# Router logits with the gates stationary in column groups, later low halves of x, and feed-forward low halves on DVE

## The chip, the core and the metric

The kernel runs on one core of a Trainium2 chip. The metric is device time in microseconds (us) for one launch, median of several runs. The engines are named as the profile names them: PE (matrix multiply), PEld (its weight load), DVE, ACT, POOL and SP (which issues most of the DMAs).

## What is computed

Three layers follow each other, and each needs the one before in full:

```python
# attention: 4 batches, 8 heads, 576 positions, head size 64
scores = scale * q @ k.T + bias            # bias: a small network on relative positions
attn = exp(scores - max) / sum
x = (attn @ v)                             # -> 2304 tokens x 512
# experts: one of 8 by the router
logits = x @ w_gate; e = argmax(logits)
gate = softmax(logits)[e] * sigmoid(x @ w_output_gate)[e]
x = gate * (relu(x @ w1[e]) @ w2[e])
# feed forward
g = x @ w_gate; out = (silu(g) * (x @ w_val)) @ w_out      # 512 -> 1536 -> 512
```

Everything is float32. Many products run as three products of halves: a float32 value a is cut into a high half h (rounded to the short format fp32r, one ACT copy) and a low half l = a - h (one subtraction), and a*b is computed as ah*bh + ah*bl + al*bh.

## The kernel before

**Attention** runs 16 units (head pair p, batch b), each of 5 steps over row pieces of 128 positions. A step makes scores on PE (line 251), the bias addition on DVE (255), the exponential on ACT (260), the transposes of the probabilities E on PE (274), their copies `pt` out of PSUM on ACT (279) and DVE (281), and the product with v on PE (336), whose result is scaled into `xT`. Units run with the batch innermost; the last head pair of batch 0 is finished in unit 13 or so, so the **router** of batch 0 can be threaded into the steps of units 14 and 15.

**The router** of batch b is a list of functions: logits (x times both gate matrices, 16 columns), `shift`, `gates`, `spread` and `first`. A table of numbers (`LG` for batch 0, `SP0` and `MC` for the first cuts of x and of the first expert weights) says at which step each function is called. For batch 0 the logits are 20 plain float32 products with x stationary and the gates moving, 16 columns wide (line 372). For the batches 1 to 3 they are 16 products of halves with `wgr`, the cut gates, stationary and 288 columns of x moving (387), then five narrow transposes (397), and an addition of the two halves. `gates` ends in two reciprocals, a maximum and three products on DVE (416 to 421), whose result `ex` is what `spread` transposes on PE (428). `first` finds the expert of the batch, `e0i`, with which SP loads that expert's weights (502, 503).

**Experts:** 4 blocks (one per batch) of 16 steps. A step is 12 products with the first weight (`T`, line 553), relu and cut (ACT 555, DVE 556), and 12 products with the second (`y`, 566). After steps 7 and 15 DVE scales four tiles of y into `yo` (575). A dictionary `todo` lists which other function is called at the end of which step: for batch b, with n = 16b - 15, router function i at step n + 4 + i//2, loads of the expert's weights from n + 7 on, their cuts (ACT 517, DVE 518) from n + 9 on. The step with the scaling of the first eight is n + 6.

**Feed forward:** five token chunks (four of 512, one of 256), each of 12 steps. In a step `gv` makes 24 products (line 1183, g and v), silu on ACT and two products on DVE (1185 to 1187), and cuts the result t into `uh` (ACT 1190) and `ul` (POOL 1191); `outs` makes the 12 products of an output piece (1205) per 128 tokens. The weights come as 36 pieces of 128 x 512 in a 64-bit format. `narrow_w` turns each into float32 and cuts it in three stages: `expo` (ACT 938), `bits` (three DVE operations, 941 to 943), `halves` (high half on ACT 946, low half on POOL 947). Pieces 0 to 5 are converted during the last expert block, pieces 6 to 35 during the steps of chunk 0, three a step, by `more_w`, which calls `cv_w` once a piece; `cv_w` runs one stage of every piece in its queue, oldest first.

All engines work through their own instructions in program order, so the order in which these functions are called is the order on each engine.

Of the kernel before, what the change touches and what calls it, by code (L numbers as in the profile page):

```python
# [21 lines left out]
NP = H // 2  # L22
# [12 lines left out]
LG = (3, 3, 5, 5, 7, 7, 8, 10, 10)  # L35
# [4 lines left out]
MC, SP0 = ((17, 18), 9)  # L40
# [67 lines left out]
def body(tc, qt, kt, va, vb, ws, moe_w_gate, moe_w_output_gate, moe_w1, moe_w2, w_gate, w_val, w_out, ctab, cst, cst2, out):  # L108
    nc = tc.nc
    with ExitStack() as ctx:  # L110
# [24 lines left out]
        wg = const.tile([128, 4, 16], F32, name="wg")  # L135
        wgr = const.tile([128, 224], F32R, name="wgr")
# [219 lines left out]
        def router(b):  # L356
# [7 lines left out]
            def logits_early(c):  # L364
                def f():
                    if c == 0:
                        t["ps"] = pO.tile([128, 512], F32, tag="pv", bufs=2, name="lps")
                        nc.gpsimd.memset(tl("lg", [128, 5, 16])[64:128, 4], 0.0)
                    ps, lg = t["ps"], t["lg"]
                    n = 64 if c == 4 else 128  # L370
                    for p in range(NP):
                        nc.tensor.matmul(ps[0:n, 16 * c:16 * c + 16], xT[p][:, b * S + 128 * c:b * S + 128 * c + n], wg[:, p],
                                         start=p == 0, stop=p == NP - 1)
                    if c == 4:
                        nc.scalar.activation(lg[:, 0:4], ps[:, 0:64].rearrange("p (c e) -> p c e", e=16), AF.Copy)
                        nc.scalar.activation(lg[0:64, 4], ps[0:64, 64:80], AF.Copy)
                return f

            def logits():

                ps = [pO.tile([128, 512], F32, tag="pv", bufs=2, name="lps") for _ in range(2)]
                t["raw"] = ap.tile([128, S], F32, tag="rb" if b else "E", bufs=1 if b else 4, name="lraw")[0:32]
                for f in range(2):
                    o = slice(288 * f, 288 * f + 288)
                    for p in range(NP):
                        for i in range(2):
                            nc.tensor.matmul(ps[f][:, 0:288], wgr[:, 32 * p:32 * p + 128], mu[b]["xs"][p][i][:, o],
                                             start=p == 0 and i == 0, stop=p == NP - 1 and i == 1)
                    nc.scalar.activation(t["raw"][:, o], ps[f][0:32, 0:288], AF.Copy)

            def logits_t():
                ps = pO.tile([128, 512], F32, tag="pv", bufs=2, name="lps")
                lg = tl("lg", [128, 5, 16])
                nc.gpsimd.memset(lg[64:128, 4], 0.0)
                for c in range(5):
                    n = 64 if c == 4 else 128
                    nc.tensor.transpose(ps[0:n, 32 * c:32 * c + 32], t["raw"][:, 128 * c:128 * c + n], ident[0:32, 0:32])
                for n, c in ((128, slice(0, 4)), (64, slice(4, 5))):
                    v = ps[0:n, 0:160].rearrange("p (c e) -> p c e", e=32)[:, c]
                    nc.scalar.activation(lg[0:n, c], v[:, :, 0:16], AF.Copy)  # L400
                    nc.vector.tensor_tensor(lg[0:n, c], v[:, :, 16:32], lg[0:n, c], ALU.add)
# [47 lines left out]
            return ([logits, logits_t] if b else [logits_early(c) for c in range(5)]) + [shift, gates, spread, first]  # L449
# [56 lines left out]
        def conv_w(raw, f):  # L506
# [9 lines left out]
            for x, y in ((a, ta), (cc, tb)):  # L516
                nc.scalar.activation(y[:, 0], x, AF.Copy)
                nc.vector.tensor_tensor(y[:, 1], x, y[:, 0].bitcast(F32), ALU.subtract)
# [228 lines left out]
        def m_conv(b, f):  # L747
            mu[b]["ws"][f] = conv_w(mu[b]["raw"][f], f)
# [20 lines left out]
        def consts():  # L769
            nc.sync.dma_start(cst_sb, cst)  # L770
            nc.sync.dma_start(wg[:, :, 0:8], moe_w_gate.rearrange("(p d) e -> d p e", p=4))
            nc.sync.dma_start(wg[:, :, 8:16], moe_w_output_gate.rearrange("(p d) e -> d p e", p=4))

        def gate_halves():
            w = wgr[:, 0:128].rearrange("p (k i e) -> p k i e", k=4, i=2)
            nc.scalar.activation(w[:, :, 0], wg, AF.Copy)
            nc.vector.tensor_tensor(w[:, :, 1], wg, w[:, :, 0].bitcast(F32), ALU.subtract)
            nc.vector.tensor_scalar(wgr[:, 128:224], ident[:, 0:96], 0.0, None, ALU.mult)
        extra.insert(len(extra) - 6, consts)
        extra.append(gate_halves)  # L780
# [149 lines left out]
        def narrow_w(n, r, t):  # L930
# [26 lines left out]
        def early_cv(n):  # L957
# [11 lines left out]
            return expo, lambda: fs[1](), lambda: fs[2]()  # L969


        p_recip(sts[15])
        late.pop()()
# [69 lines left out]
        for i in range(2):  # L1043
            t_ev(*a[0:3], t_pe(a[3], a[2], i), i)
            pvs(2)
# [69 lines left out]
        with ExitStack() as c2:  # L1115
# [39 lines left out]
            def cv_w(n):  # L1155
# [10 lines left out]
                for q in list(cvq):  # L1166
                    q.pop(0)()
                if cvq and not cvq[0]:
                    cvq.pop(0)

            us = {}

            def gv(j, f):
# [17 lines left out]
                nc.gpsimd.tensor_tensor(ul, t, uh.bitcast(F32), ALU.subtract)  # L1191
# [51 lines left out]
            def more_w(n):  # L1243
                for m in range(MW(n), min(MW(n + 1), 3 * NF + 2)):
# [3 lines left out]
                    cv_w(m)  # L1248
                for _ in range(FL):
# [3 lines left out]
            for n, (j, f) in enumerate(steps):  # L1253
# [5 lines left out]
                if j == 0:  # L1259
                    more_w(f)  # L1260
                if f == NF - 2 and j + 1 < NCH:
# [24 lines left out]
```

## Time and profile before

| | us |
|---|---|
| median of 3 runs (lowest to highest) | 1089.32 (1085.95 to 1091.72) |
| the profiled execution | 1090.41 |
| its span in the trace | 1088.6 |
| attention, units 0 to 13 (69.80 to 289.33) | 219.53 |
| attention, unit 14 (289.33 to 315.35) | 26.02 |
| attention, unit 15 and the hand-over (315.35 to 345.03) | 29.68 |
| feed forward, chunk 0 up to its last step (609.40 to 733.13) | 123.73 |
| feed forward, 35 steps behind it (733.13 to 1020.00) | 286.87 |

Over the span the granted TensorE clock is 0.969 of full speed, PE is busy 94%, DVE 52%, ACT 42%, POOL 20%. These shares are averages over stages with different limits. The stage tables give, for a stretch, the busy time of each engine; the waits view sums what an engine waited for; the timeline gives single instructions with their start and duration.

### The profile page before, as it was taken

To read this page: it belongs to the slowest core of one execution; us is meant where nothing else is said; L and a number is where in the kernel's file an instruction comes from. 1 tells how busy PE (TensorE), PEld (TensorE's weight loads), DVE (VectorE), ACT (ScalarE), POOL (GpSimd) and SP (SyncE) were. 2 spreads that over 40 slices of the span, in tenths; PEclk is the share of its full clock that TensorE was granted. 3 is DMA by queue.
4 is the path that set the end of the run, shared out by engine and by line. 5 is a ranking of instruction groups with operands and counts; after the bars stand their busy time and mean duration, and the time that the engine had idled before them with its cause. 6 is when DMAs were issued, how large, how long until landed. Compare 5 with 4: busy or idle time off the path is not lost. (4 is left out here: it accounts for less than half of the span.)

```text
span 1088.6 us, 19099 instructions
## 1 busy us (share of the span) xinstructions
PE 1027.2 (94%) x7544; PEld 818.5 (75%) x7544; DVE 562.4 (52%) x1225; ACT 457.9 (42%) x1034; POOL 217.3 (20%) x212
## 2 busy tenths in 40 slices
PE   7979999999988999999998888889999999999998
PEld 2347666666765899999998666668888888888897
DVE  8966677767645554545655599971112211211211
ACT  6766777777644433333444344442112111211221
POOL 2112333323300000000020155541111111111111
PEclk9988999999978999999999899999999999999999
DMA  6773342333012241734733544422000100100010
GB/s 191 208 249 105 95 126 84 98 115 102 2 29 71 69 156 55 278 107 130 247 120 135 188 136 155 136 77 78 1 1 20 58 1 1 58 1 1 1 39 20
DMA packets 67758, 101.94 MB, mean 94 GB/s; under 512 B 9136, under 2 KB 37936, under 8 KB 67664
## 3 DMA queue, kind: packets, MB, share of 16 engines
q1 hardware_dynamic: 67504, 100.41, 28.8%
q8 instruction: 61, 1.00, 0.4%
q14 instruction: 33, 0.27, 0.1%
q10 hardware_dynamic: 160, 0.26, 0.1%
HBM read 74.63 MB, written 26.03 MB: 92 GB/s over the span
## 5 line engine op out<-in xcount | busy, mean ns | idle before, releaser
L1183 PE MATMUL v<-x,w 128*128 128x512 f32 (+1 forms) x720 | 166.2, 379 | 16.8 <-POOL w L947 16.1
L1183 PEld LDWEIGHTS v<-x,w 128*128 128x128 f32 x720 | 128.3, 193 | 46.2 <-POOL w L947 20.4
L1183 PE MATMUL g<-x,w 128*128 128x512 f32 (+1 forms) x720 | 158.8, 369 | 2.4 <-DVE x L1146 1.5
L1186 DVE TENSOR_TENSOR t<-g,t 128x512 f32<-128x512 f32 (+1 forms) x60 | 38.2, 636 | 226.1 <-ACT t L1185 226.1
L1183 PEld LDWEIGHTS g<-x,w 128*128 128x128 f32 x720 | 126.7, 188 | 27.5 <-DVE x L1146 3.0
L1191 POOL TENSOR_TENSOR ul<-t,uh 128x512 fp32r<-128x512 f32 (+1 forms) x60 | 72.6, 1211 | 333.0 <-ACT uh L1190 333.0
L1205 PE MATMUL o<-w,uh 128*128 128x512 f32 x432 | 134.5, 393 | 0.0
L260 ACT ACTIVATE E<-E,st 128x576 f32<-128x576 f32 x144 | 110.6, 774 | 4.8 <-DVE st L255 4.4
L274 PEld LDWEIGHTS T<-ident,E 64*128 64x128 f32 x1312 | 67.6, 145 | 58.5 <-ACT pt L279 26.4
L336 PE MATMUL pv<-pt,rawv 128*64 128x256 f32 (+1 forms) x640 | 103.3, 437 | 1.3 <-DVE xT L342 1.3
L274 PE MATMUL T<-ident,E 64*128 64x64 f32 x1312 | 94.3, 243 | 9.4 <-DVE pt L281 4.0
L255 DVE CUSTOM_DVE_ANT_0 E<-S,bias 128x576 f32<-128x576 f32 x128 | 92.0, 755 | 18.9 <-PE S L251 10.8
L1185 ACT ACTIVATE t<-g 128x512 f32<-128x512 f32 (+1 forms) x60 | 33.1, 551 | 155.4 <-PE g L1183 155.4
L1190 ACT ACTIVATE uh<-t 128x512 fp32r<-128x512 f32 (+1 forms) x60 | 35.4, 589 | 146.1 <-DVE t L1187 146.1
L1205 PEld LDWEIGHTS o<-w,uh 128*128 128x128 f32 x432 | 81.4, 190 | 16.6
L281 DVE COPY pt<-T 128x256 f32<-128x256 f32 x160 | 59.6, 414 | 61.0 <-PE T L274 61.0
L279 ACT ACTIVATE pt<-T 128x320 f32<-128x320 f32 (+1 forms) x160 | 56.0, 392 | 70.2 <-PE T L274 67.8
L1205 PE MATMUL o<-w,ul 128*128 128x512 f32 x216 | 84.7, 392 | 0.0
L251 PE MATMUL S<-kh,qz 64*128 64x288 f32 (+1 forms) x576 | 79.6, 327 | 3.6 <-DVE st L255 3.1
L555 ACT ACTIVATE qz<-T 128x288 fp32r<-128x288 f32 x63 | 25.9, 411 | 103.7 <-PE T L553 103.7
L556 DVE SCALAR_TENSOR_TENSOR qz<-T,qz 128x288 fp32r<-128x288 f32 x63 | 28.8, 457 | 75.7 <-ACT qz L555 75.6
L1187 DVE TENSOR_TENSOR t<-v,t 128x512 f32<-128x512 f32 (+1 forms) x60 | 38.3, 638 | 55.6 <-PE v L1183 54.2
(246 smaller groups left out, 1741.3 us busy)
## 6 DMA issues: line engine op xcount, KB each, us to landing
raww<-in_moe_w_dram SPq DMA_DIRECT2D x16, 768.0 KB, 6.1
bscr<-ob SPq DMA_DIRECT2D x36, 288.0 KB, 3.6
bias<-bscr SPq DMA_DIRECT2D x16, 576.0 KB, 4.6
rw<-in_w_gate_dram SPq DMA_DIRECT2D x12, 512.0 KB, 3.6
rw<-in_w_val_dram SPq DMA_DIRECT2D x12, 512.0 KB, 3.6
rw<-in_w_out_dram SPq DMA_DIRECT2D x12, 512.0 KB, 3.7
rawq<-in_qt_dram SPq DMA_DIRECT2D x16, 320.0 KB, 3.3
rawk<-in_kt_dram SPq DMA_DIRECT2D x16, 288.0 KB, 2.8
```

The lines of the kernel that those rows point to most:

```text
L251: nc.tensor.matmul(t[:, f, 0:288], x[k, a], y[k, o], start=i == 0, stop=i == 2)
L255: nc.vector.tensor_tensor_reduce(out=E.rearrange("p (a b) -> p a b", a=2), in0=ps[:, :, 0:288], in1=bt[p, hh, c].rearrange("p (a b) -> p a ...
L260: nc.scalar.activation(E, E, AF.Exp, bias=st[:, 2 * c + hh:2 * c + hh + 1], scale=-1.0, accum_out=st[:, 10 + 2 * c + hh:11 + 2 * c + hh])
L274: nc.tensor.transpose(t[r][:, 64 * j:64 * j + 64], E[k, o:o + 128], ident[k, k])
L279: nc.scalar.activation(o, x, AF.Copy)
L281: nc.vector.tensor_copy(o, x)
L336: nc.tensor.matmul(st["ps"][64 * hh:64 * hh + 64, 0:w], vt[p][:, hh, b, c, :], pts[p, b][f][:, c + (5 * hh if c < 4 else 0), :], start=c = ...
L1183: nc.tensor.matmul(t, a[:, 128 * k:128 * k + 128], x, start=k == 0 and n == 0, stop=k == 3 and n == 2)
L1186: nc.vector.tensor_tensor(t, ps[0], t, ALU.mult)
L1187: nc.vector.tensor_tensor(t, ps[1], t, ALU.mult)
L1191: nc.gpsimd.tensor_tensor(ul, t, uh.bitcast(F32), ALU.subtract)
L1205: nc.tensor.matmul(ops[j][m], u[:, o], w, start=f == 0 and n == 0, stop=f == NF - 1 and n == 2)
```

## The change

Three things are changed.

**Router.** One set of functions serves all batches. The logits are 8 plain float32 products: the gates of head pair p (16 columns, filled with zeros to 32) are stationary, 288 columns of x move, and the four head pairs write into four groups of 32 PSUM partitions. ACT copies 128 partitions twice, PE transposes five 128 x 128 pieces, and DVE adds up the four groups with two reductions. The cut gates `wgr` and their three instructions are gone. `gates` is cut into `gates` and `gates_2`; with seven functions instead of six, batches 1 to 3 run `gates_2` and `spread` at step n + 6 and `first` at n + 7. For batch 0 the table now puts the logits into step 0 of unit 14.

**First cuts of x.** The cuts of x of batch 0 are called one step later (`SP0`), the low halves of the first expert weight are put off into a list, and that list and the reciprocal of the last unit are called between the two halves of the transposes behind unit 15.

**Feed forward.** The low halves of weight pieces and of the products u are subtracted on DVE instead of POOL. A piece has four stages, and `cv_w` runs: high half of piece m-2 (ACT), bits of m-1 (DVE), low half of m-2 (DVE), `expo` of m (ACT). `ul` is put off into `pend` and called after the first `cv_w` of the next `more_w`.

```diff
-LG = (3, 3, 5, 5, 7, 7, 8, 10, 10)
+LG = (1, 5, 5, 7, 8, 10, 10)
-MC, SP0 = ((17, 18), 9)
+SP0 = (10, 12, 14, 16, 17)
...
             def logits():
-                ps = [pO.tile([128, 512], F32, tag="pv", bufs=2, name="lps") for _ in range(2)]
+                ps = [pO.tile([128, 512], F32, tag="pv", bufs=2, name="lps") if b else t_tile() for _ in range(2)]
...
                     for p in range(NP):
-                        for i in range(2):
-                            nc.tensor.matmul(ps[f][:, 0:288], wgr[:, 32 * p:32 * p + 128], mu[b]["xs"][p][i][:, o],
-                                             start=p == 0 and i == 0, stop=p == NP - 1 and i == 1)
-                    nc.scalar.activation(t["raw"][:, o], ps[f][0:32, 0:288], AF.Copy)
+                        nc.tensor.matmul(ps[f][32 * p:32 * p + 32, 0:288], wg[:, p], x_src(p, b)[:, o], start=True, stop=True)
+                    nc.scalar.activation(t["raw"][:, o], ps[f][:, 0:288], AF.Copy)
...
+            def gates_2():
+                ex, sm, oh = t["ex"], t["sm"], t["oh"]
                 nc.vector.reciprocal(ex[:, :, 8:16], ex[:, :, 8:16])
...
-            return ([logits, logits_t] if b else [logits_early(c) for c in range(5)]) + [shift, gates, spread, first]
+            return [logits, logits_t, shift, gates, gates_2, spread, first]
...
-            q += [(g + SP0 + i, f) for i, f in enumerate(mu[0]["sp"][0:8])]
-            q += [(g + MC[i], lambda i=i: m_conv(0, i)) for i in range(2) if MC[i] < 18]
+            q += [(g + SP0[(i + 1) // 2], f) for i, f in enumerate(mu[0]["sp"][0:8])]
+            q += [(g + SP0[4], lambda: m_conv(0, 0, lows))]
...
-                nc.gpsimd.tensor_tensor(l, t, h.bitcast(F32), ALU.subtract)
-            return expo, bits, halves
+
+            def low():
+                nc.vector.tensor_tensor(l, t, h.bitcast(F32), ALU.subtract)
+            return expo, bits, halves, low
...
-        p_recip(sts[15])
-        late.pop()()
...
-        for i in range(2):
-            t_ev(*a[0:3], t_pe(a[3], a[2], i), i)
-            pvs(2)
+        t_ev(*a[0:3], t_pe(a[3], a[2], 0), 0)
+        p_recip(sts[15])
+        late.pop()()
+        for f in lows:
+            f()
+        pvs(2)
+        t_ev(*a[0:3], t_pe(a[3], a[2], 1), 1)
+        pvs(2)
...
-                for q in list(cvq):
+                old = [q for q in cvq if len(q) == 2]
+                mid = [q for q in cvq if len(q) == 3]
+                new = [q for q in cvq if len(q) == 4]
+                for q in old + mid + old + new:
                     q.pop(0)()
...
-                nc.gpsimd.tensor_tensor(ul, t, uh.bitcast(F32), ALU.subtract)
+                pend.append(lambda: nc.vector.tensor_tensor(ul, t, uh.bitcast(F32), ALU.subtract))
...
                     cv_w(m)
+                    lows()
```

What stands on DVE in one step of chunk 0 of the feed forward, before (`rw` and `tw` are a piece in its 64-bit form and in work, `g` and `v` the products in PSUM, `t` their silu product):

```order
L1186 TENSOR_TENSOR t<-g,t 128x512
L1187 TENSOR_TENSOR t<-v,t 128x512
L941 TENSOR_SCALAR rw<-rw 128x512
L942 SCALAR_TENSOR_TENSOR tw<-tw,rw 128x512
L943 SCALAR_TENSOR_TENSOR tw<-rw,tw 128x512
```

The same place after:

```order
L1182 TENSOR_TENSOR t<-g,t 128x512
L1183 TENSOR_TENSOR t<-v,t 128x512
L925 TENSOR_SCALAR rw<-rw 128x512
L926 SCALAR_TENSOR_TENSOR tw<-tw,rw 128x512
L927 SCALAR_TENSOR_TENSOR tw<-rw,tw 128x512
L933 TENSOR_TENSOR w_8855<-tw,w_8855 128x512
L1187 TENSOR_TENSOR ul<-t,uh 128x512
```

The three operations of `bits` stand three times in a step in both; a subtraction of a weight's low half now follows each of them, and one of `ul` the first. On POOL these 36 and 60 subtractions are gone.

DVE in an expert block, at the end of the step whose y products are scaled, before (`oh`, `ex`, `sm` belong to the router, `qz` is the cut relu, `cn` counts tokens for `first`):

```order
L416 RECIPROCAL ex<-ex 128x5x8
L417 RECIPROCAL sm<-sm 128x5
L418 TENSOR_REDUCE sm<-oh 128x5
L419 TENSOR_TENSOR oh<-oh,sm 128x40
L420 TENSOR_TENSOR ex<-oh,sm 128x5x8
L421 TENSOR_TENSOR ex<-ex 128x5x8
L556 SCALAR_TENSOR_TENSOR qz_116<-T,qz_116 128x288
L575 TENSOR_TENSOR yo<-y,gb 128x288 x4
L441 SCALAR_TENSOR_TENSOR cn<-cn,cst_sb 1x8
```

The same place after:

```order
L396 SCALAR_TENSOR_TENSOR oh<-lg,cst_sb 128x40
L545 SCALAR_TENSOR_TENSOR qz_115<-T,qz_115 128x288
L564 TENSOR_TENSOR yo<-y,gb 128x288 x4
L400 RECIPROCAL ex<-ex 128x5x8
L401 RECIPROCAL sm<-sm 128x5
L402 TENSOR_REDUCE sm<-oh 128x5
L403 TENSOR_TENSOR oh<-oh,sm 128x40
L404 TENSOR_TENSOR ex<-oh,sm 128x5x8
L405 TENSOR_TENSOR ex<-ex 128x5x8
```

The six operations that end in `ex` stood ahead of the four scalings and now stand behind them; PE's transposes of `ex` keep their place in PE's order.

PE at the first logits of batch 0, in unit 14, before (`lps` are the logits in PSUM, `T` a tile for transposes):

```order
L336 MATMUL pv<-pt_4249,rawv 64x256 x2
L372 MATMUL lps<-wg,xT_812 128x16
L372 MATMUL lps<-wg,xT_1808 128x16
L372 MATMUL lps<-wg,xT_2893 128x16
L372 MATMUL lps<-wg,xT_3979 128x16
L274 MATMUL T<-ident,E 128x64 x8
```

The same place after:

```order
L335 MATMUL pv<-pt_4246,rawv 64x256 x4
L370 MATMUL T<-xT_809,wg 32x288
L370 MATMUL T<-xT_1805,wg 32x288
L370 MATMUL T<-xT_2890,wg 32x288
L370 MATMUL T<-xT_3976,wg 32x288
L273 MATMUL T<-ident,E 128x64 x8
```

Such four rows with `lps` stand five times before, in three steps; the 20 products of 16 columns (40 passes in the trace, two for a float32 product) are replaced by eight of 288 columns with 32 stationary columns each, of which the first four are shown.

## Rows read from the trace of the kernel before

**Rows 1.** Stage table: stretch, length, busy by engine, PEclk, DMA share, GB/s.

```profile
69.80:289.33 219.53, 211.91 (x2534) 145.39 (x2531) 152.90 (x439) 157.90 (x440) 69.34 (x86) 0.97 0.33 104
289.33:315.35 26.02, 24.63 (x228) 18.65 (x226) 12.33 (x43) 11.98 (x36) 5.20 (x7) 0.74 0.01 2
315.35:345.03 29.68, 24.34 (x239) 15.30 (x237) 16.47 (x54) 15.58 (x45) 1.82 (x5) 0.84 0.29 90
609.40:733.13 123.73, 106.67 (x421) 82.29 (x421) 108.83 (x120) 53.23 (x91) 63.70 (x43) 0.94 0.45 141
733.13:1020.00 286.87, 285.90 (x1260) 236.02 (x1259) 56.75 (x82) 53.50 (x91) 44.25 (x35) 1.00 0.07 21
```

**Rows 2.** Waits of PE over the whole span: us in total, times, longest.

```profile
PE v L1183 <- POOL w L947: 16.1, 10, 2.0
...
PE T L274 <- DVE pt L281: 4.0, 4, 1.9
```

**Rows 3.** Timeline of PE at the last of the ten waits: start, duration.

```profile
726.37 0.96 PE L1183 MATMUL v<-x,w 128*128 128x512 f32 x3 [2.03 <-POOL w L947]
```

**Rows 4.** Timeline of DVE in chunk 0: the first piece, then one step.

```profile
617.66 1.07 DVE L941 TENSOR_SCALAR rw<-rw 128x512 int32<-128x512 int32 x1 [1.25 <-ACT tw L938]
...
644.60 0.68 DVE L1186 TENSOR_TENSOR t<-g,t 128x512 f32<-128x512 f32 x1
...
645.99 0.42 DVE L941 TENSOR_SCALAR rw<-rw 128x512 int32<-128x512 int32 x1
646.51 0.69 DVE L942 SCALAR_TENSOR_TENSOR tw<-tw,rw 128x512 int32<-128x512 int32 x1
647.24 1.67 DVE L943 SCALAR_TENSOR_TENSOR tw<-rw,tw 128x512 int32<-128x512 int32 x1
...
652.07 0.69 DVE L943 SCALAR_TENSOR_TENSOR tw<-rw,tw 128x512 int32<-128x512 int32 x1
652.68 0.42 DVE L941 TENSOR_SCALAR rw<-rw 128x512 int32<-128x512 int32 x1
...
655.52 0.68 DVE L1186 TENSOR_TENSOR t<-g,t 128x512 f32<-128x512 f32 x1
```

**Rows 5.** Timeline of POOL in the same step.

```profile
646.88 1.48 POOL L1191 TENSOR_TENSOR ul<-t,uh 128x512 fp32r<-128x512 f32 x1 [2.76 <-ACT uh L1190]
648.33 3.16 POOL L947 TENSOR_TENSOR w<-tw,w 128x512 fp32r<-128x512 f32 x2
```

**Rows 6.** Timeline of DVE: two such subtractions on DVE, in the expert stage.

```profile
366.73 1.28 DVE L518 TENSOR_TENSOR whl<-raww,whl 128x512 fp32r<-128x512 f32 x2
```

**Rows 7.** Timeline of PE at the border of two chunks.

```profile
831.96 1.43 PE L1183 MATMUL g<-x,w 128*128 128x512 f32 x5 [0.49 <-DVE x L1146]
```

**Rows 8.** Timeline of PE: logits of batch 0 in unit 14, 16 passes.

```profile
303.23 3.60 PE L372 MATMUL lps<-wg,xT 128*128 128x16 f32 x16
```

**Rows 9.** Timeline of PE, bias stage: four float32 products (eight passes), 32 stationary columns each.

```profile
48.80 1.06 PE L814 MATMUL bps<-zk,small 128*32 128x512 f32 x8
```

**Rows 10.** Timeline of the router of batch 1 and its expert's weights.

```profile
374.13 0.29 PE L387 MATMUL lps<-xh,wgr 128*128 128x288 f32 x1
...
376.35 0.31 PE L397 MATMUL lps<-ident,lraw 32*128 32x32 f32 x2
...
381.27 0.40 DVE L416 RECIPROCAL ex<-ex 128x40 f32<-128x40 f32 x1
...
382.28 0.20 DVE L421 TENSOR_TENSOR ex<-ex 128x40 f32<-128x40 f32 x1
...
383.12 1.54 DVE L575 TENSOR_TENSOR yo<-y,gb 128x288 f32<-128x288 f32 x4
...
383.63 0.74 PE L428 MATMUL gps<-ident,ex 128*8 128x128 f32 x5
...
394.09 0.63 ACT L517 ACTIVATE w2hl<-raww 128x512 fp32r<-128x512 f32 x1 [0.16 <-DMA raww<-in_moe_w_dram]
...
396.18 0.41 ACT L555 ACTIVATE qz<-T 128x288 fp32r<-128x288 f32 x1 [1.46 <-PE T L553]
```

More of the change, by code (lines that the diff above doesn't have):

```diff
@@ L362, in tl @@
                 return t[name]
[L364 to L377, printed above, removed]
             def logits():
-                ps = [pO.tile([128, 512], F32, tag="pv", bufs=2, name="lps") for _ in range(2)]
-                t["raw"] = ap.tile([128, S], F32, tag="rb" if b else "E", bufs=1 if b else 4, name="lraw")[0:32]
+                ps = [pO.tile([128, 512], F32, tag="pv", bufs=2, name="lps") if b else t_tile() for _ in range(2)]
+                t["raw"] = ap.tile([128, S], F32, tag="rb" if b else "E", bufs=1 if b else 4, name="lraw")
                 for f in range(2):
@@ L385, in logits @@
                     for p in range(NP):
-                        for i in range(2):
-                            nc.tensor.matmul(ps[f][:, 0:288], wgr[:, 32 * p:32 * p + 128], mu[b]["xs"][p][i][:, o],
-                                             start=p == 0 and i == 0, stop=p == NP - 1 and i == 1)
-                    nc.scalar.activation(t["raw"][:, o], ps[f][0:32, 0:288], AF.Copy)
+                        nc.tensor.matmul(ps[f][32 * p:32 * p + 32, 0:288], wg[:, p], x_src(p, b)[:, o], start=True, stop=True)
+                    nc.scalar.activation(t["raw"][:, o], ps[f][:, 0:288], AF.Copy)
             def logits_t():
-                ps = pO.tile([128, 512], F32, tag="pv", bufs=2, name="lps")
+                ps = [pO.tile([128, 512], F32, tag="pv", bufs=2, name="lps") if b else t_tile() for _ in range(2)]
                 lg = tl("lg", [128, 5, 16])
@@ L396, in logits_t @@
                     n = 64 if c == 4 else 128
[L397 to L401, printed above, removed]
+                    nc.tensor.transpose(ps[c // 4][0:n, 128 * (c % 4):128 * (c % 4) + 128], t["raw"][:, 128 * c:128 * c + n], ident)
+                for n, c, i in ((128, slice(0, 4), 4), (64, slice(4, 5), 1)):
+                    v = ps[c.start // 4][0:n, 0:128 * i].rearrange("p (c g e) -> p c e g", c=i, g=4)
+                    nc.vector.tensor_reduce(lg[0:n, c], v[:, :, 0:16], AX.X, ALU.add)
             def shift():
@@ L504, in load_w, with conv_w @@
             return [(a[:, :, 128 * i:128 * i + 128], c[:, i]) for i in range(n)]
-        def conv_w(raw, f):
+        lows = []
+        def conv_w(raw, f, later=None):
             a, c = raw
@@ L517, in conv_w @@
                 nc.scalar.activation(y[:, 0], x, AF.Copy)
-                nc.vector.tensor_tensor(y[:, 1], x, y[:, 0].bitcast(F32), ALU.subtract)
+                if later is None:
+                    nc.vector.tensor_tensor(y[:, 1], x, y[:, 0].bitcast(F32), ALU.subtract)
+                else:
+                    later.append(lambda x=x, y=y: nc.vector.tensor_tensor(y[:, 1], x, y[:, 0].bitcast(F32), ALU.subtract))
             return ta, tb
@@ L745, in m_load_f, with m_conv @@
             m["raw"].append((a, c))
-        def m_conv(b, f):
-            mu[b]["ws"][f] = conv_w(mu[b]["raw"][f], f)
+        def m_conv(b, f, later=None):
+            mu[b]["ws"][f] = conv_w(mu[b]["raw"][f], f, later)
         def m_gate(b):
@@ L968, in expo @@
                 fs[0]()
-            return expo, lambda: fs[1](), lambda: fs[2]()
-        p_recip(sts[15])
-        late.pop()()
+            return expo, lambda: fs[1](), lambda: (fs[2](), fs[3]())
         pvq = [f for n in sorted(pe) for f in pe[n]]
@@ L1165, in cv_w, with lows @@
                     cvq.append(list(narrow_w(n, rw.pop(n), wp.tile([128, 512], F32, tag="tw", bufs=3, name="tw"))))
-                for q in list(cvq):
+                old = [q for q in cvq if len(q) == 2]
+                mid = [q for q in cvq if len(q) == 3]
+                new = [q for q in cvq if len(q) == 4]
+                for q in old + mid + old + new:
                     q.pop(0)()
-                if cvq and not cvq[0]:
-                    cvq.pop(0)
+                cvq[:] = [q for q in cvq if q]
             us = {}
+            pend = []
+            def lows():
+                while pend:
+                    pend.pop(0)()
             def gv(j, f):
@@ L1260, in body @@
                     more_w(f)
+                lows()
                 if f == NF - 2 and j + 1 < NCH:
```

10 lines of the change are left out of this document (2 added, 8 removed).

## The prediction

> **What bounds the kernel now.** I read the stage table first, since the averages of the page mix stages, then PE's waits, then the timelines of the stretches that the change touches. The stage table [rows 1] shows three kinds of stretch. Behind chunk 0 of the feed forward PE is busy 285.90 of 286.87 us at a clock of 1.00: nothing that another engine does faster shortens them. In chunk 0 PE is busy only 106.67 of 123.73 us and DVE 108.83, its highest share in the table; the waits view says whom PE waits for: ten times, 16.1 us in all, for a weight's low half from POOL [rows 2]. In units 14 and 15 nobody is full, and the granted clock is 0.74 and 0.84, so part of that time runs at the lower of the two levels (1.2 instead of 2.4 GHz); PE also waits four times, 4.0 us, for DVE's copies of the transposes there [rows 2]. The change reaches all of these except the chunks behind chunk 0. Terms are worked against the profiled run, 1090.41 us.
>
> **A. Feed forward, chunk 0.** The wait names POOL, but POOL is fed by DVE, so I read DVE's step. It lasts 10.92 us, from one product of g to the next (644.60 to 655.52), without idle time [rows 4]. In it the same operation has two durations: the third of `bits` takes 0.69 us at 652.07 and 1.67 at 647.24. The long one begins beside POOL's subtraction of `ul` (646.88, 1.48 us) and ends when its next ones, of weights, have begun (648.33, 3.16 us for two); at 652.07 these are over [rows 5]. I read this as DVE being held up while POOL subtracts. What a step costs DVE undisturbed comes from the short pitches [rows 4]: two products 1.39 (644.60 to 645.99); of a piece, first operation to second 0.52 (645.99 to 646.51), second to third 0.73 (646.51 to 647.24), third to the next 0.61 (652.07 to 652.68), together 1.86. Three pieces and two products are 5.58 + 1.39 = 6.97. The other 3.95 us of the step fall to POOL's four subtractions, 0.99 each.
>
> On DVE such a subtraction of 128 x 512 costs 0.64 us (two in 1.28 [rows 6]); the bounds are 0.61 and 0.73, the pitches above of the same shape. So each subtraction adds 0.64 where it now takes 0.99. The new step is 6.97 + 4 x 0.64 = 9.53 us. PE does not become the limit: its 36 products a step at full speed, 0.228 us each (1260 in 286.87 us [rows 1]), are 8.2 us. To get the end, I count DVE's work from its first piece (617.66 [rows 4]) to the low half for which PE now resumes at 726.37 [rows 3], that of piece 34: one `ul`, 30 pieces of bits, ten pairs of products, 29 low halves and nine more `ul`. That is 617.66 + 0.64 + 55.8 + 13.9 + 38 x 0.64 = 712.3. Against 726.4 this is **-14.0** us; with 0.73 a subtraction it is -10.6, with 0.61 and the first piece's 1.07 us operation shortened as well -16. Loads of raw pieces do not come in between: the DMA engines are 45% busy in this stage [rows 1], and SP's order is as before. The order of the two kernels shows that no feed-forward subtraction is left on POOL, so that the change does not do what it says is ruled out.
>
> What is late next is again DVE: PE will wait for its low halves. In later chunks a `ul` on DVE has room (56.75 us of DVE work in 286.87 [rows 1]).
>
> **B. Chunk borders.** At the start of a chunk PE waits 0.49 us for DVE's low half of x [rows 7], which shares its time with POOL's `ul`. Three such borders; I take -1.2, between 0 and -1.5.
>
> **C. Unit 14.** Units 0 to 13 take 219.53 us for 70 steps, 3.14 a step [rows 1]. Unit 14 takes 26.02 where five steps would be 15.7: 10.3 us too many. The 20 small logit products have most of it: they are 40 passes in the trace, of which 16 take 3.60 us [rows 8] where the clock is low. They go. New are eight products of 288 columns. In the bias stage four such products of 512 columns, also with 32 stationary columns in a PSUM group each, take 1.06 us for their eight passes [rows 9]; one after another, at 0.228 a pass, they would take 1.8, so they overlap. Eight of 288 are then 8 x 0.265 x 288/512 = 1.2, or 2.4 where the clock is at half. Then five transposes of 128 columns, two copies of 128 partitions on ACT and two reductions on DVE, and the logits stand right after the batch's last `xT`, so the fourth of them waits for DVE, and the next transposes for ACT's copies. I leave 3.5 us of the excess (1 to 7): **-6.8**, at best -9.3, and -3 if the clock still falls.
>
> **D. Unit 15 and the hand-over.** The low halves of x move one step back, and those of the first weight and the last reciprocal behind the first transposes' copies, so that DVE's copies stand in front. That removes the waits of 4.0 us [rows 2]; I take -3.5, and -1.5 for the clock, which at 0.84 cost more than that [rows 1]: **-5**, between -2 and -9. What is moved comes due only with the first expert products, and DVE is busy 16.47 of 29.68 us there [rows 1].
>
> **E. Expert blocks 1 to 3.** The logits now take 2.22 us of PE (374.13 to 376.35 [rows 10]) and will take about 1.2 [rows 9]: -1.0 each, -3 in all. Against that, `gates_2` now stands behind the four scalings of `yo`. These end at 383.12 + 1.54 = 384.66; the six operations take 1.21 us (381.27 to 382.28 + 0.20), so `ex` is there at 385.87, while PE starts its transposes at 383.63 [rows 10]. In DVE's queue nothing urgent stands behind, but in PE's the next step's 12 products do. PE waits 2.24 us in each of the three blocks: **+6.7**. `first` and with it SP's weight loads come one step later. Now the second weight lands 0.16 us after ACT is ready for it (394.09); a load that is 4 us later, against a cut 2.2 us later, stops ACT for some 2 us. Behind it in ACT's queue stands the relu (396.18), which now idles 1.46 us before PE has finished [rows 10], and its result is needed a step after: I take nothing, and up to 1 us a block as the bound. Together **+3.7**, between +2.9 and +9.
>
> **Costed at nothing:** the three instructions on the cut gates (in the bias stage, beside other DVE and ACT work), the six early low halves (the last expert block has DVE idle in every step), the last `ul`.
>
> Sum: -14.0 - 1.2 - 6.8 - 5 + 3.7 = -23.3, so 1067.1 us for a run like the profiled one. The median lies 1.1 us below that run: **1066**.
>
> **Rivals.**
> *The clock stays low in units 14 and 15.* The new logits still put waits on PE where the clock is 0.74 now. Then C is -3 and D -2, the sum -16.5: 1073. For it speaks that the clock is already below 1 in two stretches; against it that the sparse 16-column products are gone.
> *DVE waits for the high halves.* Each low half now needs ACT's copy, which may stand in ACT's queue behind a silu that waits for PE. If each of the 38 subtractions waited 0.36 us, all of A would be lost: 1080. Against it: 1.86 us of bits stand ahead of each subtraction, and ACT is busy only 53.23 of 123.73 us [rows 1].
> *Everything at its best:* A -16, B -1.5, C -9.3, D -9, E +2.9: 1056.
> *Slower: the long operations are DVE's own.* If the 1.67 us have nothing to do with POOL (a conflict with a DMA into the same memory, say), nothing is freed, and DVE gets four subtractions more a step: 10.92 + 2.56 = 13.48, over 9.9 steps +25 instead of -14. With the other terms this is 1105. The point from which it decides: when a subtraction costs DVE more than the 0.99 us that its removal from POOL frees. Against it speak the times of the long operations, which begin with POOL's [rows 4, 5].
>
> The Trainium skill, "Perfetto Trace Analysis", section Optimizing Scalar/DVE Operations, says that with a saturated DVE, giving work to Scalar or even GPSIMD may make sense. By that, moving it back to DVE in chunk 0 loses, and the time would be that of this rival, 1105. The section adds that DVE and GPSIMD share a read port, so that giving work from one to the other may not help; the trace agrees with this half, with 0.69 us against 1.67 for one operation [rows 4].
>
> **How the numbers follow.** Forecast 1066 with 0.58; low clock 1073 with 0.20; waits for high halves 1080 with 0.10; everything at its best 1056 with 0.07; slower 1105 with 0.05. The range 1055 to 1079 leaves out the slower case, half of the 1080 and of the 1056 case and little of the rest. About 0.5%, 5.4 us, is what a measurement of this kernel can tell from no change: faster means below 1083.9, slower above 1094.8. The first, second and fourth case are all faster, and most of the third: 0.92; of the third 0.03 stays within 0.5%; slower 0.05.
>
> **What would show it.** A: all operations of `bits` at 0.42 or 0.69 us, DVE's step near 9.5 us, PE's waits in chunk 0 for DVE, no longer for POOL, and chunk 0 some 14 us shorter. B: no wait at the borders. C: a clock near 1.0 in unit 14 and a length near 19 us. D: PE's waits for `pt` gone. E: three waits of PE of about 2.2 us at the transposes of `ex`. Wrong would be: third operations of `bits` that stay at 1.67 us without POOL; waits of DVE for ACT's high halves; a clock that stays at 0.74; PE waiting in the expert blocks for weights that came late.

## The result

The changed kernel takes 1062.11 us (median of 4, 1060.66 to 1066.1) against 1089.47 us of the kernel before: a ratio of 0.9757 (95% interval 0.9719 to 0.9796), 27 us less. The forecast was 1066 (1055 to 1079). The profiled execution took 1061.21 us, its span is 1059.0 us, 29.6 less than that of before.

The stage table of the changed kernel, from the same events as before: first scores, first transposes of unit 14, of unit 15, transposes just ahead of the first expert product; then first product of g, first of chunk 1, and 35 steps behind it (stretch, length, busy times, PEclk, DMA share, GB/s):

```profile
67.47:287.92 220.45, 211.27 (x2530) 144.59 (x2531) 152.86 (x439) 157.74 (x440) 70.53 (x87) 0.97 0.33 103
287.92:306.80 18.88, 18.00 (x211) 11.46 (x209) 13.25 (x46) 12.48 (x36) 5.14 (x7) 1.00 0.01 2
306.80:327.58 20.78, 19.52 (x237) 12.77 (x235) 16.81 (x53) 15.64 (x45) 2.17 (x5) 1.00 0.44 129
601.10:705.54 104.44, 100.15 (x420) 77.56 (x421) 95.63 (x161) 52.96 (x90) 0.04 (x1) 1.00 0.54 167
705.54:992.00 286.46, 286.46 (x1263) 236.68 (x1262) 79.47 (x117) 54.31 (x92) 0.00 (x0) 1.00 0.07 21
```

Beside [rows 1] it says where the 29.6 us went, by the events that limit each stage:

| stage | before | after | difference | forecast |
|---|---|---|---|---|
| bias, up to the first scores | 69.9 | 67.5 | -2.4 | 0 |
| units 0 to 13 | 219.5 | 220.4 | +0.9 | 0 |
| unit 14 | 26.0 | 18.9 | -7.1 | -6.8 |
| unit 15 and hand-over | 29.7 | 20.8 | -8.9 | -5 |
| expert blocks and small rest | 264.4 | 273.5 | +9.1 | +3.7 |
| feed forward, chunk 0 | 123.7 | 104.4 | -19.2 | -14.0 |
| feed forward behind it and end | 355.5 | 353.5 | -2.0 | -1.2 |

Every forecast term has the sign that was forecast, but three sizes are off: chunk 0 and unit 15 gave more, and the expert blocks took back 9 us where 3.7 were expected. The +0.9 us of units 0 to 13 belong to this one execution: by the same events they take 219.3 and 219.4 us in the two kernels of the section on units 14 and 15. The waits of PE over the changed kernel (us in total, times, longest) show both sides:

```profile
PE gps L412 <- DVE ex L405: 6.4, 3, 2.1
...
PE v L1179 <- DVE w L933: 3.8, 8, 0.5
...
PE T L273 <- DVE pt L280: 0.3, 1, 0.3
```

The wait for a low half fell from 16.1 us for POOL to 3.8 for DVE, that for `pt` from 4.0 to 0.3 [rows 2], and a new one stands at the top: three times 2.1 us for `ex`.

### The profile page after: what moved, and what is told of

The parts are those of the page before. It is cut to its first block, busy times and chain, and to the rows that moved or that the text cites. A ratio compares the mean times of both kernels' runs of the same rounds, so it can differ in the third digit from the quotient of the medians.

```text
span 1059.0 us, 18936 instructions
## 1 busy us (share of the span) xinstructions
PE 1008.8 (95%) x7525; PEld 802.9 (76%) x7525; DVE 577.9 (55%) x1321; ACT 457.5 (43%) x1027; POOL 117.1 (11%) x117
## 5 line engine op out<-in xcount | busy, mean ns | idle before, releaser
L1179 PE MATMUL v<-x,w 128*128 128x512 f32 (+1 forms) x720 | 161.1, 371 | 4.1 <-DVE w L933 3.8
L1179 PEld LDWEIGHTS v<-x,w 128*128 128x128 f32 x720 | 124.9, 189 | 32.3 <-DVE w L933 7.5
L273 PEld LDWEIGHTS T<-ident,E 64*128 64x128 f32 x1312 | 65.4, 140 | 55.5 <-ACT pt L278 27.4
L335 PE MATMUL pv<-pt,rawv 128*64 128x256 f32 (+1 forms) x640 | 99.3, 423 | 0.0
L273 PE MATMUL T<-ident,E 64*128 64x64 f32 x1312 | 92.0, 237 | 6.2 <-ACT rb L323 3.6
L1201 PEld LDWEIGHTS o<-w,uh 128*128 128x128 f32 x432 | 80.3, 188 | 16.1
L250 PEld LDWEIGHTS S<-kh,qz 64*128 64x128 f32 (+1 forms) x576 | 54.8, 192 | 8.0 <-DVE st L254 5.9
```

The lines of the kernel that those rows point to most:

```text
L250: nc.tensor.matmul(t[:, f, 0:288], x[k, a], y[k, o], start=i == 0, stop=i == 2)
L273: nc.tensor.transpose(t[r][:, 64 * j:64 * j + 64], E[k, o:o + 128], ident[k, k])
L335: nc.tensor.matmul(st["ps"][64 * hh:64 * hh + 64, 0:w], vt[p][:, hh, b, c, :], pts[p, b][f][:, c + (5 * hh if c < 4 else 0), :], start=c = ...
L1179: nc.tensor.matmul(t, a[:, 128 * k:128 * k + 128], x, start=k == 0 and n == 0, stop=k == 3 and n == 2)
L1201: nc.tensor.matmul(ops[j][m], u[:, o], w, start=f == 0 and n == 0, stop=f == NF - 1 and n == 2)
```

## The experiments

### Each part by itself

Two kernels take the feed-forward part apart from the rest: one is the kernel before with that part alone, the other the changed kernel without it.

```diff
 # feed forward alone: the kernel before, and in it
-                nc.gpsimd.tensor_tensor(l, t, h.bitcast(F32), ALU.subtract)
-            return expo, bits, halves
+
+            def low():
+                nc.vector.tensor_tensor(l, t, h.bitcast(F32), ALU.subtract)
+            return expo, bits, halves, low
... (cv_w with its four stages)
-                nc.gpsimd.tensor_tensor(ul, t, uh.bitcast(F32), ALU.subtract)
+                pend.append(lambda: nc.vector.tensor_tensor(ul, t, uh.bitcast(F32), ALU.subtract))
```

> The kernel before with the feed-forward part of the change alone. Theory: chunk 0 loses 19.2 us (123.7 to 104.4) and the chunks behind 2.1, as in the changed kernel: 1089.5 - 21.3 = 1068.2 us. Rival (part of the faster chunk 0 comes from the other two parts of the change, through an earlier and undisturbed start): chunk 0 shortens by the predicted 14 us or less, 1074 us or more.

> The changed kernel with the feed-forward part undone (low halves on POOL, three stages). Theory: units 14 and 15 keep their gain of 16 us, the expert blocks their loss of 9 us, chunk 0 is 123.7 us again: 1062.1 + 21.3 = 1083.4 us. Whether the 2.4 us by which the bias stage was shorter belong to the change shows here too: with its cause in the dropped gate halves the first scores start near 67.5 us again; by chance, anywhere between 67.5 and 70.

Measured: 1071.89 us (1069.7 to 1073.54) alone, a ratio of 0.9834 (0.9793 to 0.9876); 1082.12 (1079.8 to 1083.98) without, 0.9927 (0.9901 to 0.9952). The two gains, 18.0 and 7.7 us, add up to 25.7 of the 27. The first lies 3.7 us above its forecast and 2.1 below the rival, so the traces have to decide. Chunk 0 takes 104.0 us in the one and 123.7 in the other, the chunks behind 2.1 us less in the one and the same as before in the other: the whole of the feed forward's gain belongs to its part, no other part helps. The kernel with that part alone has, with the cut gates still in it, its first scores at 68.2 us; in the changed kernel and all other runs here they stand between 67.3 and 68.7, in the profiled run of before at 69.9. So most of the 2.4 us of the bias stage is that one execution (its clock is 0.83 between 60 and 70 us, where it is 1.00 in the changed kernel), not the change.

### POOL's subtractions and DVE

The prediction read the long DVE operations as held up by POOL. Two runs put one kind of subtraction back on POOL and leave everything else.

```diff
 # u on POOL
-                pend.append(lambda: nc.vector.tensor_tensor(ul, t, uh.bitcast(F32), ALU.subtract))
+                nc.gpsimd.tensor_tensor(ul, t, uh.bitcast(F32), ALU.subtract)
 # weights on POOL
             def low():
-                nc.vector.tensor_tensor(l, t, h.bitcast(F32), ALU.subtract)
+                nc.gpsimd.tensor_tensor(l, t, h.bitcast(F32), ALU.subtract)
```

> The changed kernel with the 60 ul subtractions back on POOL, those of the weights on DVE. Theory (POOL's subtraction holds DVE's two-input operations up by some 0.98 us): of a chunk 0 step, 9.19 us on DVE in the changed kernel, 0.60 goes and 0.98 comes: 9.57, over some ten steps +4 us; the chunk borders get back their waits, +2; about 1068 us. Rival (the long operations are DVE's own and POOL's are free): DVE's step is 8.6, chunk 0 a few us shorter, 1060 us or less.

> The changed kernel with the weights' low halves back on POOL (still a stage of their own), ul on DVE. Theory (POOL holds DVE up): three subtractions a step at 0.98 instead of 0.60, +0.38 x 29 = +11 us in chunk 0, none at the borders behind, about 1073 us. Rival (POOL's subtractions are free for DVE): DVE's step falls by 1.8 us, PE becomes the bound at about 8.2 us a step and chunk 0 loses up to 8 us, 1054 us.

Measured: 1069.79 us (1068.93 to 1071.77) with `ul` on POOL, 1074.68 (1072.59 to 1075.68) with the weights on POOL; both slower than the changed kernel, as the theory has it. DVE's step in chunk 0 is 9.56 us with `ul` on POOL, where 9.57 was forecast, and chunk 0 takes 4.6 us more (4 forecast). With the weights on POOL the step is 10.73 us and chunk 0 takes 14.7 us more, where 11 were forecast: two of the three operations held up in a step lose 1.08 us and not 0.98. DVE's timeline with `ul` on POOL (start, duration), then POOL's:

```profile
645.34 0.70 DVE L926 SCALAR_TENSOR_TENSOR tw<-tw,rw 128x512 int32<-128x512 int32 x1
646.07 1.67 DVE L927 SCALAR_TENSOR_TENSOR tw<-rw,tw 128x512 int32<-128x512 int32 x1
647.66 0.68 DVE L933 TENSOR_TENSOR w<-tw,w 128x512 fp32r<-128x512 f32 x1
...
649.43 0.69 DVE L927 SCALAR_TENSOR_TENSOR tw<-rw,tw 128x512 int32<-128x512 int32 x1
```

```profile
645.78 1.41 POOL L1187 TENSOR_TENSOR ul<-t,uh 128x512 fp32r<-128x512 f32 x1 [8.15 <-ACT uh L1186]
```

Of the three third operations of `bits` in a step only the one that starts while POOL subtracts is long, and it ends 0.55 us behind POOL's end (647.74 against 647.19), where it takes 0.69 by itself. So it does not run slower beside POOL, it stands still until POOL is done. With the weights on POOL the same befalls the operations that begin at that moment:

```profile
646.66 1.76 DVE L1187 TENSOR_TENSOR ul<-t,uh 128x512 fp32r<-128x512 f32 x1
648.34 1.50 DVE L925 TENSOR_SCALAR rw<-rw 128x512 int32<-128x512 int32 x1
649.94 0.69 DVE L926 SCALAR_TENSOR_TENSOR tw<-tw,rw 128x512 int32<-128x512 int32 x1
```

```profile
646.15 3.41 POOL L933 TENSOR_TENSOR w<-tw,w 128x512 fp32r<-128x512 f32 x2 [3.21 <-ACT w L930]
```

A subtraction (0.68 alone) takes 1.76 and the first operation of `bits` (0.42 alone) 1.50: about 1.08 us lost each. Not every DVE operation is held up, though. In the kernel before, from the expert blocks on, all 48 operations that begin beside a POOL subtraction and have their tensor inputs in SBUF end behind it. Those with an input in PSUM take their usual time: the 28 bias additions that begin beside one take 0.75 to 0.76 us, as the other 116 do, and a product with g takes 0.69. That settles the rival of operations that are long by themselves. The Trainium skill, "SBUF — State Buffer", section SBUF: two separate sides, says that GpSimd and DVE operations with two SBUF inputs, or in a mode that uses both of its ports, take a shared pair of ports under an exclusive lock, and the later one blocks fully; the traces agree, with 0.98 to 1.08 us lost to a POOL subtraction of 1.41 to 1.7.

### The low half directly behind the high half

```diff
-                for q in old + mid + old + new:
+                for q in old + old + mid + new:
```

> The changed kernel with a piece's low half called directly behind its high half, ahead of the bits of the next piece. Theory: the 1.8 us of bits that stand ahead of each low half are what hides ACT's copy of the high half; without them DVE waits about 0.8 us (the copy and the signal) for most of the 29 low halves, chunk 0 gets 15 to 23 us longer, 1077 to 1085 us. Rival (the order does not matter, ACT is always ahead): 1062 us.

Measured: 1084.25 us (1081.87 to 1086.95), 22 us more than the changed kernel, and chunk 0 takes 126.9 us, more than before the change. DVE's waits in the stretch from 600 to 715 us, then its timeline, then ACT's:

```profile
DVE w L933 <- ACT w L930: 17.4, 19, 1.2
```

```profile
637.59 0.69 DVE L933 TENSOR_TENSOR w<-tw,w 128x512 fp32r<-128x512 f32 x1 [0.70 <-ACT w L930]
...
640.78 0.69 DVE L1183 TENSOR_TENSOR t<-v,t 128x512 f32<-128x512 f32 x1
642.69 0.69 DVE L933 TENSOR_TENSOR w<-tw,w 128x512 fp32r<-128x512 f32 x1 [1.21 <-ACT w L930]
643.30 0.42 DVE L925 TENSOR_SCALAR rw<-rw 128x512 int32<-128x512 int32 x1
```

```profile
641.51 0.63 ACT L1186 ACTIVATE uh<-t 128x512 fp32r<-128x512 f32 x1 [2.90 <-DVE t L1183]
642.05 0.61 ACT L930 ACTIVATE w<-tw 128x512 fp32r<-128x512 f32 x1
```

The low half waits for ACT's copy of the high half. Where the bits of the piece have only just ended, the wait is 0.70 us. Where the products of g and v stand between, it is 1.21 us, because in ACT's queue the copy stands behind that of `uh`, which needs the product with v. A third piece in each step has `ul` between and waits for nothing. So the move to DVE pays only with the order that comes with it: the bits of the next piece between a piece's high half on ACT and its low half on DVE. Without that order the kernel is no faster than the changed kernel without its whole feed-forward part (1082.12 us). With the change's order DVE has no such wait.

### Units 14 and 15

```diff
 # old x: the second part of the change undone
-            q += [(g + SP0[(i + 1) // 2], f) for i, f in enumerate(mu[0]["sp"][0:8])]
-            q += [(g + SP0[4], lambda: m_conv(0, 0, lows))]
+            q += [(g + 9 + i, f) for i, f in enumerate(mu[0]["sp"][0:8])]
+            q += [(g + 17, lambda: m_conv(0, 0))]
... (the last reciprocal back ahead of the transposes, nothing put off)
 # old logits: 20 products of 16 columns for batch 0, in three steps
-LG = (1, 5, 5, 7, 8, 10, 10)
+LG = (3, 3, 5, 5, 7, 7, 8, 8, 10, 10)
... (logits_early as in the kernel before)
-            return [logits, logits_t, shift, gates, gates_2, spread, first]
+            return ([logits, logits_t] if b else [logits_early(c) for c in range(5)]) + [shift, gates, gates_2, spread, first]
```

> The changed kernel with the second part undone: x's first cuts a step earlier and one by one, the first weight's low halves not put off, the last reciprocal ahead of the transposes. Theory: unit 15 and the hand-over lose the whole of what they gained (29.7 to 20.8 us): PE waits for DVE's copies of pt again, about 4 us, the clock falls behind the waits, +8.9, 1071 us. Rival (most of that gain comes from the logits, which leave unit 15 a running clock): +4 or less, 1066 us.

> The changed kernel with the logits of batch 0 as before: 20 products of 16 columns, spread over three steps of unit 14. Theory: unit 14 takes 26 us again instead of 18.9, with a clock near 0.74, unit 15 stays at about 21: 1069 us. Rival (the products are not it, the clock falls only together with the waits of unit 15 or by the work around): unit 14 stays below 21 us, 1064 us.

Measured: 1071.73 us (1069.85 to 1072.57) with the old x, 1068.13 (1065.54 to 1070.58) with the old logits. The stage tables, unit 14 and then unit 15 with the hand-over; first the old x, then the old logits:

```profile
287.01:305.89 18.88, 18.00 (x209) 11.43 (x207) 13.24 (x46) 12.46 (x36) 5.13 (x7) 1.00 0.01 2
305.89:335.19 29.30, 24.07 (x237) 15.01 (x236) 16.40 (x53) 15.63 (x45) 1.80 (x5) 0.83 0.31 92
```

```profile
287.31:313.32 26.01, 24.62 (x228) 18.70 (x227) 12.33 (x43) 11.97 (x36) 5.20 (x7) 0.74 0.01 2
313.32:334.10 20.78, 19.52 (x237) 12.77 (x235) 16.85 (x54) 15.58 (x45) 2.16 (x5) 1.00 0.43 129
```

The two gains are separate and add up: the old x gives unit 15 back its length (29.3) and its clock (0.83) and leaves unit 14 alone, the old logits the other way round (26.0 and 0.74). Neither rival holds. PE's waits between 285 and 346 us with the old x name the cause again:

```profile
PE T L273 <- DVE pt L280: 4.0, 4, 1.9
```

The old x lengthens the stage by 8.5 us: PE waits about 4 us more, and is busy 24.07 us instead of 19.52 for as many instructions, at a clock of 0.83. Which of the moves in this part (the cuts of x, the low halves put off, the reciprocal) takes the waits away is not shown, since the run undoes them together.

In unit 14 the old logits lower the clock without a wait of PE ahead. The stretches of the run with the old logits, cut where the clock changes, then PE's timeline:

```profile
287.31:295.60 8.29, 8.29 (x106) 6.43 (x106) 4.85 (x15) 5.81 (x18) 5.20 (x7) 1.00 0.01 2
295.60:309.25 13.65, 12.32 (x86) 9.51 (x85) 4.74 (x13) 3.88 (x11) 0.00 (x0) 0.50 0.00 1
```

```profile
293.29 1.96 PE L371 MATMUL lps<-wg,xT 128*128 128x16 f32 x16
295.18 0.47 PE L273 MATMUL T<-ident,E 64*128 64x64 f32 x8
```

PE is busy in all of the first 8.29 us. The last long piece of work before the fall is the 16 passes of the old logits, and then 13.65 us run at 0.50. So most of the 7.1 us of unit 14 is clock, not the products' own time: 16 of their passes take 1.96 us at full clock, and the 12.32 us of work in the slow stretch would take some 6 us less at twice the clock (an estimate). What in the old logits lets the clock fall is not shown, since no run varies their shape alone.

### The three waits in the expert blocks

In the changed kernel the half blocks in which the router ends take 30.4 us from one scaling of `yo` to the next in the first two blocks, 26.6 before (the third: 33.5 and 29.6). The stretches of the changed kernel behind the first such scaling:

```profile
364.59:368.60 4.01, 1.87 (x22) 1.25 (x21) 2.56 (x11) 0.51 (x2) 0.00 (x0) 1.00 0.01 2
368.60:372.00 3.40, 3.40 (x15) 3.40 (x16) 0.00 (x0) 0.65 (x4) 0.00 (x0) 0.52 0.03 5
372.00:376.00 4.00, 4.00 (x32) 4.00 (x31) 1.86 (x10) 0.41 (x1) 0.11 (x1) 0.98 0.22 15
```

and PE's timeline there:

```profile
367.39 0.74 PE L412 MATMUL gps<-ident,ex 128*8 128x128 f32 x5 [2.14 <-DVE ex L405]
```

PE waits 2.14 us, as forecast (2.24), and then runs 3.4 us at a granted clock of 0.52, the lower of its two levels: 15 products where the stretch behind it has 32 in 4.0 us. That is some 1.7 us more per block, which the prediction did not count.

The run with the old logits of batch 0 shows the wait without the slow stretch, in its first block (PE's timeline, then the two stretches behind the scaling):

```profile
375.41 0.74 PE L427 MATMUL gps<-ident,ex 128*8 128x128 f32 x5 [2.15 <-DVE ex L420]
```

```profile
372.59:376.60 4.01, 1.86 (x22) 1.25 (x21) 2.57 (x11) 0.50 (x2) 0.00 (x0) 1.00 0.01 2
376.60:380.00 3.40, 3.40 (x26) 3.40 (x27) 1.07 (x7) 0.67 (x4) 0.00 (x0) 1.00 0.05 10
```

The wait is the same, the clock stays at 1.00, 26 products run in the next 3.40 us instead of 15, and the half block takes 28.9 us: 2.3 more than 26.6, where it is 3.8 with the slow stretch. It is the only one of the 21 such waits in the seven kernels with the late `gates_2` behind which the clock does not fall.

The late loads are the other candidate for the 1.7 us; two more runs tell them apart. The first calls `gates_2` directly behind `gates`, the second too, but leaves `first` and the loads where the change has them.

```diff
-            for i, f in enumerate(router(b)):
-                at(n + 4 + i // 2, f)
+            for k, f in zip((4, 4, 5, 5, 5, 6, 6), router(b)):    # (4, 4, 5, 5, 5, 6, 7) with first late
+                at(n + k, f)
```

The two added lines give the order of both runs in short; the kernels write it a little differently.

> The changed kernel with gates_2 called directly behind gates in batches 1 to 3, so that its six DVE operations stand ahead of the four yo scalings again and first comes a step earlier. Theory: in the changed kernel PE waits 2.14 us for ex in each of three blocks, and the clock of 0.52 in the 3.4 us behind the wait costs another 1.7; both go, the half blocks with the router return from 30.4 to 26.6 us, and the time is 1062.1 - 3 x 3.8 = 1050.7 us. Rival: the extra 1.7 us a block are something else that the split does not cause; then only the waits go and the time is about 1055.7.

> As the run with gates_2 ahead of the yo scalings, but first, and with it the loads of the expert's weights, stays a step later as in the changed kernel. Theory (wait and clock): the late loads make ACT wait some 1.3 us for two weights but nothing on PE, so the time is that of the other run, 1050.7 us. Rival (late weights cost the extra 1.7 us a block): 5 us more, about 1055.7.

Measured: 1050.6 us (1047.81 to 1054.3), ratio 0.9645 (0.9602 to 0.9689), and 1051.19 (1049.16 to 1051.98). The three half blocks take 26.57, 26.58 and 29.59 us in the first (30.40, 30.42 and 33.48 in the changed kernel), 26.58, 26.58 and 29.96 in the second. PE's transposes of `ex` start without a wait:

```profile
364.55 1.54 DVE L564 TENSOR_TENSOR yo<-y,gb 128x288 f32<-128x288 f32 x4
365.06 0.74 PE L412 MATMUL gps<-ident,ex 128*8 128x128 f32 x5
```

With `first` late ACT does wait for its two weights, as the sum had it, and PE does not wait for them; in the third block PE waits 0.27 us for the count in `first`, and that half block is 0.4 us longer. ACT's waits with `first` late, between 364 and 396 us:

```profile
ACT w2hl L503 <- DMA raww<-in_moe_w_dram: 1.5, 1, 1.5
ACT w1hl L503 <- DMA raww<-in_moe_w_dram: 0.8, 1, 0.8
```

So the loss is wait and clock, and calling `gates_2` a step later is what costs it; without that the change gives 39 us instead of 27.

### The six early low halves

While the pieces 0 to 5 are converted, the half block that began at 523.04 us before grew from 33.30 to 34.2 us in the runs that have these six low halves on DVE, and PE has a wait there that before has not (changed kernel):

```profile
PE y L555 <- DVE qz L545: 0.6, 1, 0.6
```

They stand in DVE's queue there ahead of a relu's low half. The run without the feed-forward part and the one with the weights on POOL have 33.3 us. This run puts those six alone back on POOL, with `gates_2` ahead:

```diff
-        def narrow_w(n, r, t):
+        def narrow_w(n, r, t, eng=nc.vector):      # early_cv passes nc.gpsimd
...
-                nc.vector.tensor_tensor(l, t, h.bitcast(F32), ALU.subtract)
+                eng.tensor_tensor(l, t, h.bitcast(F32), ALU.subtract)
```

> The changed kernel with gates_2 ahead of the yo scalings, and with the low halves of weight pieces 0 to 5 (converted in the last expert block) on POOL as in the kernel before. Theory: PE's wait of 0.6 us for a relu's low half in the last expert block goes, that half block falls from 34.2 to 33.3 us, all else is as in the run with gates_2 ahead (1050.6): 1049.7 us. Rival (POOL's subtractions hold DVE up there as they do in chunk 0): the half block stays at 34.2 or grows, 1050.6 us or more.

Measured: 1050.1 us (1048.61 to 1050.4), ratio 0.9644 (0.9607 to 0.9682). In the trace the half block is 33.28 us again and the wait is gone; in the time 0.5 us cannot be told from nothing. The rival is half right, as POOL's row and DVE's show:

```profile
526.05 2.97 POOL L933 TENSOR_TENSOR w<-rw,w 128x512 fp32r<-128x512 f32 x2 [1.95 <-ACT w L930]
```

```profile
526.13 1.76 DVE L927 SCALAR_TENSOR_TENSOR rw<-rw 128x512 int32<-128x512 int32 x1
527.81 0.45 DVE L545 SCALAR_TENSOR_TENSOR qz<-T,qz 128x288 fp32r<-128x288 f32 x1
```

POOL does hold up an operation of `bits` (1.76 us), but not the relu's low half, which has an input in PSUM and for which PE would wait. This is the fastest of the kernels here, 12 us ahead of the changed kernel, together with the run that only has `gates_2` ahead.

## Why the prediction was right, and where it was off

**A, chunk 0: mechanism right, size short.** DVE's step is 9.19 us in the changed kernel (9.53 forecast):

```profile
631.83 0.68 DVE L1182 TENSOR_TENSOR t<-g,t 128x512 f32<-128x512 f32 x1
...
633.22 0.42 DVE L925 TENSOR_SCALAR rw<-rw 128x512 int32<-128x512 int32 x1
...
635.02 0.69 DVE L933 TENSOR_TENSOR w<-tw,w 128x512 fp32r<-128x512 f32 x1
635.62 0.68 DVE L1187 TENSOR_TENSOR ul<-t,uh 128x512 fp32r<-128x512 f32 x1
636.23 0.42 DVE L925 TENSOR_SCALAR rw<-rw 128x512 int32<-128x512 int32 x1
...
641.02 0.69 DVE L1182 TENSOR_TENSOR t<-g,t 128x512 f32<-128x512 f32 x1
```

A subtraction adds 0.60 us (635.02 to 635.62), not 0.64, and the bits of a piece 1.80 (633.22 to 635.02), not 1.86. From the first product of g to the end of the last wait for a low half it is 99.3 us instead of 116.9: -17.6 where the sum had -14.0 and its bound -16. The bound failed because it counted the first `ul` as work in the chain, which lies in a pause ahead of the first piece, and took 1.86 as fixed. The remaining 1.6 of the 19.2 us come behind that wait: the 23 products up to the first of chunk 1 took 6.76 us at a clock of 0.75 before and take 5.12 now. The sum had left the clock of this stage out, though [rows 1] showed 0.94. As to the rivals, the high halves are indeed ready in time, for the reason given (the run without the bits between shows it), and the long operations were POOL's. The slower rival is out: the feed-forward part by itself gained 18.0 us.

**B, borders: right in its cause, beyond its bound of -1.5.** PE has no wait behind chunk 0 any more (0.49, 0.49 and 0.34 us before), and it is -2.0 with the end of the span, against -1.2. With `ul` back on POOL it is 356.2 us from chunk 1 to the end of the span, with `ul` on DVE and the weights on POOL 353.4: it is `ul` alone. A border with a wait of 0.49 cost 0.65 us; the sum had only the waits.

**C, unit 14: right in size**, -7.1 against -6.8, clock 1.00. The sum put most of the excess down to the small products; their 40 passes took 6.2 us of the 26.0, and most of the rest of the excess was the clock that fell behind the first 16. The eight products' 16 passes take longer than the 1.2 us that the sum has for a full clock, in unit 14 though not in the expert blocks (first unit 14, then the first expert block):

```profile
290.69 1.81 PE L370 MATMUL T<-xT,wg 128*32 128x288 f32 x16
...
356.64 1.18 PE L370 MATMUL lps<-xT,wg 128*32 128x288 f32 x16
```

The clock is 1.00 in both; why unit 14 has 1.81 is not shown.

**D, unit 15: right in its cause, short by 4 us.** The waits were valued at 3.5 us and the clock behind them at 1.5; the run with the old x shows 8.5 us, of which 4.5 are PE's slower work at the lower clock. The range for it, 2 to 9, held it.

**E, expert blocks: the wait was right to 0.1 us, its price was not.** The logits gave -0.9 a block where -1.0 was forecast (28.56 to 27.63 us in the half blocks that have them). The wait was priced at its own length, 2.24; it costs 3.8 with the slow stretch behind it, and 2.3 in the one block that has none. The sum had a term for the clock beside PE's waits in unit 15 and carried none over to this place; the term was given "up to +9" for late weights, which cost at most 0.4 us, in one block.

**Costed at nothing:** the cut gates, of which no cost shows, rightly; the early low halves cost 0.9 us.

The errors had both signs (+5.4 in E, -5.2 in A, -3.9 in D, -2.4 in the bias stage, most of it chance). That 1066 lies within 4 us of the measured 1062.1 is in part luck: had E come out as forecast and the rest as measured, it would have been about 1056.7, near the end of the range.

## What to carry to other kernels

A wait of PE for another engine costs more than its length when the clock falls behind it: 3.8 us for 2.14 here, 8.5 for some 4 in unit 15. The clock does not fall behind every wait: it stayed at 1.00 at the chunk borders (0.49 us each), and before the change only four stretches of 3.4 us in chunk 0 were slow with ten waits of 16.1 us together. So price a wait between its length and twice that, and look first at what a split or a delay puts behind other work on an engine that PE waits for. When DVE is the bound of a stage, look at what POOL does there: a POOL subtraction of 128 x 512 took 0.98 to 1.08 us from a DVE operation with its inputs in SBUF, and on DVE itself it cost 0.60. Here moving it paid only because the operand from a third engine (ACT's high half) was ready in time, with other work of DVE put between.

## What the runs showed of the hardware

The granted clock was 0.52, 0.52 and 0.51 in the 3.40 us of full work behind the three waits of PE of 2.1 us each, though it had been 1.00 up to each of them; with the old logits it stayed at 1.00 behind one such wait of 2.15. It also fell without a wait, to 0.50 for 13.65 us, right behind the 16 passes of the old logits in unit 14. DVE operations with their inputs in SBUF that begin beside a POOL subtraction stand still until it ends, whether they have one tensor input (0.42 becomes 1.50 us, ending 0.28 behind POOL) or two (0.68 becomes 1.76, ending 0.55 behind POOL). Those with an input in PSUM are not held up (0.45 us in 2.97 us of POOL's subtractions).
